# Batch 0's softmax, the fused weights and the weight conversions of a fused attention and feed-forward kernel get due times of their own

## The chip, the cores and the metric

The kernel runs on one core of a Trainium2 chip. The metric is the device time of one launch in microseconds (us), inputs and output in DRAM; all is computed in float32 precision. A core has TensorE (PE), VectorE (DVE), ScalarE (ACT), GpSimd (POOL), and SyncE (SP), which issues all transfers here; DMA engines carry them.

## The reference

```python
def _attn_ref(q, k, v, tau) -> np.ndarray:          # (4, 6080, 256)
    qn = q / (np.linalg.norm(q, axis=1, keepdims=True) + 1e-06)
    kn = k / (np.linalg.norm(k, axis=1, keepdims=True) + 1e-06)
    s = kn.transpose(0, 2, 1) @ qn / tau
    s = s - s.max(-1, keepdims=True)
    a = np.exp(s)
    a /= a.sum(-1, keepdims=True) + 1e-09
    return (v @ a).astype(np.float32)
...
    h = x @ w_in                                     # 256 -> 2048
    h2 = h * h
    h3 = h2 * h
    P = a[0] + a[1] * h + a[2] * h2 + a[3] * h3
    Q = 1.0 + np.abs(b[0]) * np.abs(h) + np.abs(b[1]) * h2
    g = P / (Q + 1e-06)
    return (g @ w_out).astype(np.float32)            # 2048 -> 256
```

The attention is over channels: for each of four batches the scores are a 256 x 256 matrix, summed over all 6080 rows of k and q. The result goes through a feed-forward layer whose activation is a quotient of polynomials.

## The kernel before, in words

**Algebra.** The matrix a of a batch is multiplied into w_in first: a *fused weight* is w_in transposed with the exponentials, scaled by the inverse of their sums. With it, v needs one matrix product to the hidden layer. The hidden layer's 2048 columns are worked as eight *pairs* of 2 x 128; so each batch has eight fused weights, each as a high and a low half (tiles w and w2), and each product is three: high x high, high x low, low x high.

**Tokens.** A batch's 6080 rows are 12 *groups*: eleven of 512 tokens and one of 448. For each group v is loaded (vst), transposed on DVE (cv) and split into vhi (ACT) and vlo (POOL). For each group and pair, `pair` then does: first product on PE into a PSUM slot hx (12 matmuls of 512 columns); on ACT the size, its square, the slope, the inverse root and its square; on DVE num, gh (high), back and rest; on POOL gl (low); and on PE the second product into acc with gh (8 matmuls) and gl (4). There are 384 pairs. `finish` transposes acc to orow and stores it.

**Attention.** `Attn` loads k and q in 24 *halves* of a batch (tile kq; in batch 0 also r). Each half gives 8 matmuls on PE and squares on ACT (tile sq), added up on POOL, and in batch 0 every fourth on DVE (the total is in orow for batch 0, in ssq for the others). `softmax` then makes norms of k and q (a matmul with ones), scores, exponentials, transposes, and calls `fuse` for each pair: 8 matmuls into an hx slot, the high half on ACT, the low half on DVE. Batch b + 1's attention runs while batch b's pairs do. Its first `FRONT` halves, for batch 1, have their products in batch 0's opening and one sum in acc.

**Weights.** `piece` turns one of 16 blocks of the float64 weights that are read as words (8 of w_in, 8 of w_out) into float32: a load into d, an absolute value on ACT, and six DVE steps in an hx slot (for w_out a high half on ACT and a low half on DVE besides). Twelve of the pieces are done in the opening.

**Order.** Nothing runs in the order in which it is written. Each `step` has an engine, an estimated cost and a due time (its key); the `Planner` plays all engines through with these costs, and gives an engine that is free the ready step with the lowest key whose buffers are free:

```python
        FIFO = ("d", "uu", "r", "gh", "gl", "w", "kq", "sq", "cv", "vst", "vhi", "vlo", "orow", "acc")
```

Tiles of these names are given out in order of key. The order that comes out is the program order of each engine; the hardware then waits on semaphores, whatever the planner thought. Due times come from two tables: `LAG` gives each operation of a pair an offset for each of the eight pairs, added to the pair's own time `at + p * II` (`II` is 3.576), and `TIME` gives the rest. The numbers are no microseconds of the chip; only their order counts. PSUM holds three hx slots and one acc. All work goes through one helper, so that the trace gives line L56 for all of it; tiles tell what is what.

In the softmax before, all steps of a batch have keys within one unit after `at`, the halves of k and q are evenly spaced, the eight fused weights are 1.116 apart, and a piece's load and conversion are 5.42 apart.

## Time and profile before

| | us |
|---|---|
| median of 3 runs | 2459.4 (2458.28 to 2464.83) |
| the profiled execution | 2459.0 |
| its span (first to last instruction) | 2457.2 |
| PE busy in it | 2370.8 |
| DVE, ACT, POOL busy | 2177.2, 2156.1, 1330.9 |

The span is what the trace covers; 1.8 us of the profiled execution lie around it. A busy PE is not the same as a PE at full clock: a matmul at a lower granted clock is busy for longer. Opening means the time until batch 0's pairs run evenly, about the first 217 us; the changes of batch lie near 680, 1270 and 1860 us.

### The profile page before, as it was taken

Reading aid. Unit: us, or ns where it says so; the run is one execution under the profiler, and the core shown is the slowest. Engines: PE = TensorE matmul, PEld = TensorE weight load, DVE = VectorE, ACT = ScalarE, POOL = GpSimd, SP = SyncE. Lnnn points to the kernel's source line nnn. Section 1 sums busy time; section 2 is a strip of 40 time slices with the busy share of each in tenths; the row PEclk is TensorE's granted clock in tenths of the full one; section 3 lists DMA queues with packets and bytes.
Section 4 is the critical chain, followed back from the end, with each engine's and each line's share of the span. In section 5 each row is a group of like instructions: output and inputs, shape, how many; then the busy total and the mean of one; then the engine's idle time right before and its main releaser. Section 6 shows DMA issues by size and latency. Waiting matters only on the chain. (4 is left out here: it accounts for less than half of the span.)

```text
span 2457.2 us, 29203 instructions
## 1 busy us (share of the span) xinstructions
PE 2370.8 (96%) x10280; PEld 1939.5 (79%) x10280; DVE 2177.2 (89%) x1953; ACT 2156.1 (88%) x2187; POOL 1330.9 (54%) x525
## 2 busy tenths in 40 slices
PE   8789999999989999999999999999999999999997
PEld 6667888888877888888878788888887778888886
DVE  7779999999978888899987888899998899999997
ACT  5488999999888888899988888889997999999996
POOL 6566555554536666554544666655553345455553
PEclk9889999999999999999999999999999999999999
DMA  9532111111112222311111223211111111111101
GB/s 315 158 106 52 22 22 26 27 25 18 26 17 52 56 56 72 72 25 18 26 18 17 61 52 77 67 18 26 25 27 18 17 26 26 18 27 26 25 9 18
DMA packets 457037, 110.04 MB, mean 45 GB/s; under 512 B 405168, under 2 KB 453808, under 8 KB 456880
## 3 DMA queue, kind: packets, MB, share of 16 engines
q1 hardware_dynamic: 456880, 108.07, 20.1%
q8 instruction: 83, 1.36, 0.2%
q14 instruction: 74, 0.61, 0.1%
HBM read 83.10 MB, written 24.90 MB: 44 GB/s over the span
## 5 line engine op out<-in xcount | busy, mean ns | idle before, releaser
L56 POOL TENSOR_TENSOR gl<-d,r 128x1024 fp32r<-128x1024 f32 (+1 forms) x384 | 957.1, 2496 | 989.2 <-DVE d L56 561.7
L56 PE MATMUL hx<-vhi,w 128*128 128x512 f32 (+1 forms) x3072 | 894.2, 393 | 7.1 <-DVE d L56 6.9
L56 PEld LDWEIGHTS hx<-vhi,w 128*128 128x128 f32 x3072 | 575.7, 188 | 141.6 <-DVE d L56 9.0
L56 DVE SCALAR_TENSOR_TENSOR hx<-uu,fit,hx 128x1024 f32<-128x1024 f32 (+1 forms) x384 | 488.0, 1271 | 89.0 <-ACT uu L56 88.7
L56 DVE SCALAR_TENSOR_TENSOR gh<-hx,fit,r 128x1024 fp32r<-128x1024 f32 (+1 forms) x384 | 485.1, 1263 | 76.3 <-ACT r L56 73.1
L56 DVE SCALAR_TENSOR_TENSOR d<-d,gh 128x1024 f32<-128x1024 f32 (+1 forms) x384 | 525.9, 1370 | 2.6
L56 ACT ACTIVATE d<-hx 128x1024 f32<-128x1024 f32 (+1 forms) x384 | 388.7, 1012 | 156.7 <-PE hx L56 134.2
L56 PE MATMUL acc<-gh,w_high 128*128 128x512 f32 (+1 forms) x1536 | 482.8, 396 | 14.7 <-DVE gh L56 10.6
L56 DVE SCALAR_TENSOR_TENSOR d<-hx,fit,d 128x1024 f32<-128x1024 f32 (+1 forms) x384 | 485.3, 1264 | 6.7
L56 PE MATMUL hx<-vlo,w 128*128 128x512 f32 (+1 forms) x1536 | 478.6, 393 | 0.0
L56 PE MATMUL acc<-gh,w_low 128*128 128x512 f32 (+1 forms) x1536 | 476.1, 391 | 0.0
L56 ACT ACTIVATE uu<-hx,fit 128x1024 f32<-128x1024 f32 (+1 forms) x384 | 457.4, 1191 | 0.0
L56 ACT ACTIVATE d<-d,fit 128x1024 f32<-128x1024 f32 (+1 forms) x384 | 437.4, 1140 | 0.0
L56 ACT ACTIVATE r<-d 128x1024 f32<-128x1024 f32 (+1 forms) x384 | 403.6, 1052 | 26.3 <-ACT d L56 0.8
L56 PE MATMUL acc<-gl,w_high 128*128 128x512 f32 (+1 forms) x1536 | 407.8, 392 | 2.9 <-POOL gl L56 2.9
L56 ACT ACTIVATE r<-r 128x1024 f32<-128x1024 f32 (+1 forms) x384 | 402.2, 1048 | 5.3
L56 PEld LDWEIGHTS acc<-gh,w_high 128*128 128x128 f32 x1536 | 289.6, 189 | 77.6 <-DVE gh L56 13.0
L56 PEld LDWEIGHTS acc<-gl,w_high 128*128 128x128 f32 x1536 | 288.0, 188 | 68.5 <-POOL gl L56 5.3
L56 PEld LDWEIGHTS acc<-gh,w_low 128*128 128x128 f32 x1536 | 290.7, 189 | 61.7
L56 PEld LDWEIGHTS hx<-vlo,w 128*128 128x128 f32 x1536 | 288.9, 188 | 63.8
L56 POOL TENSOR_TENSOR ssq<-sq,ssq 128x1024 f32<-128x1024 f32 (+1 forms) x69 | 186.7, 2706 | 82.2 <-ACT sq L56 80.3
L56 POOL TENSOR_TENSOR vlo<-cv,vhi 128x1024 fp32r<-128x1024 f32 (+1 forms) x48 | 149.4, 3112 | 18.5 <-ACT vhi L56 18.5
(107 smaller groups left out, 1017.5 us busy)
## 6 DMA issues: line engine op xcount, KB each, us to landing
vst<-in_v_dram SPq DMA_DIRECT2D x352, 64.0 KB, 2.4
out_dram<-orow SPq DMA_DIRECT2D x352, 64.0 KB, 1.9
kq<-in_k_dram SPq DMA_DIRECT2D x78, 256.0 KB, 3.5
kq<-in_q_dram SPq DMA_DIRECT2D x78, 256.0 KB, 4.1
d<-in_moe_w_in_dram SPq DMA_DIRECT2D x8, 512.0 KB, 6.3
r<-in_k_dram SPq DMA_DIRECT2D x10, 256.0 KB, 5.8
r<-in_q_dram SPq DMA_DIRECT2D x10, 256.0 KB, 6.1
d<-in_moe_w_out_dram SPq DMA_DIRECT2D x4, 512.0 KB, 6.8
```

Of the source, the lines that this page charges most:

```text
L56: ins = op(*args, **kwargs)
```

## The change

1. The numbers of `LAG` and `TIME` are others. New entries give a due time to each piece's load and each piece's conversion (`piece_load`, `piece`), to each fused weight (`fuse0` in batch 0, `turn` in the others), to each step of the softmax (`chain0`, `chain`), to the first v (`value0`), and an offset to each pair of the first group (`first`), of the first group of a later batch (`opening`) and of the last group of a batch (`last`).
2. `FRONT` goes from 12 to 6: of batch 1's halves, six instead of twelve have their products in the opening.
3. In `softmax` the DVE step that folded the two sums of squares into one is gone; PE does the norms of both sums and adds them in PSUM. The maximum, y and the corrected norms stay in PSUM (nps); scores and exponentials are written into the tile of the squares' sum instead of two sq slots; the transposed exponentials (eT) and rk have buffers of their own. Tiles n2 and y are gone.
4. Costs that the planner takes for these steps are others.

Of the tables, a few lines stand for all.

```diff
...
-    "high": (-0.201, -1.824, -3.214, 1.127, -2.441, -0.333, -0.417, 2.742),
...
+    "high": (22.59291, 24.11209, 24.41897, 24.49546, 24.51312, 23.95582, 24.16201, 24.16013),
...
-    "out0": -1.882, "out": -2.395, "attn0_0": -6.63, "attn_0": 0.275, "attn0": 6.33, "attn": 1.996,
-    "attn1": 92.175, "value": 148.575, "fuse": 1.116, "finish": 72.482, "front": 29.573,
...
+    "pair": 3.576, "start": 175.73828, "load": 0.04809, "softmax": 4.9627, "in": 5.42,
...
+    "attn0": 6.54104, "attn": 0.29516, "attn1": 93.92602, "value": 201.67145, "finish": 125.06256,
+    "front": 75.0448, "front_pace": 13.10818,
...
+    "fuse0": (167.64562, 152.54228, 165.11912, 148.87503, 168.34446, 172.36125, 175.0073, 179.5675),
+    "turn": (-37.56063, -0.4301, -46.60573, 6.0525, 1.56793, 0.10546, 5.12072, 16.26872),
+    "first": (-0.04097, -23.90782, -16.14628, -4.63735, -4.34016, -4.78556, -4.65507, -5.66606),
+    "last": (-1.36381, -1.49737, 4.25864, -3.87953, 4.30997, 4.5312, -4.86916, 2.06908),
+    "opening": (1.54538, 7.26692, 6.40396, 11.04622, 3.47761, -3.70507, -6.7909, -1.11722),
...
+    "value0": -8.75639, "ahead": 49.0606, "vhi": -95.57053, "vlo": 79.4786,
...
-    FRONT = 12
+    FRONT = 6
...
-              "n2": C + NC2, "s0": C + NC2, "y": C + NC2, "e": C + NC2}
+              "s0": C + NC2, "e": C + NC2, "rk": NC2, "eT": 2 * C}
...
+                chain = TIME["chain" if b else "chain0"]
                 nps = buf("hx", [P, 2, GT], F32, "norms")
-                n2, s0, y, e = (buf(t, [P, W], F32) for t in ("n2", "s0", "y", "e"))
-                rn, rk = (buf(t, [P, W], F32, "r" + t) for t in ("y", "n2"))
+                s0, e = buf("s0", [P, W], F32), buf("e", [P, W], F32)
                 total = self.ssq
 
-                def fold():
-                    dve.tensor_tensor(total[:, : 2 * C], total[:, : 2 * C], total[:, 2 * C :], op=ALU.add)
-
                 def norms_pe():
-                    pe.matmul(nps[:, 0, 0:C], ones, total[:, C : 2 * C], start=True, stop=True, skip_group_check=True)
-                    for i in range(NC2):
+                    for n in range(2):
+                        at = 2 * n * C
                         pe.matmul(
-                            nps[:, 0, C + i : C + i + 1], total[:, i * P : (i + 1) * P], ones[:, 0:1],
-                            start=False, stop=True, skip_group_check=True,
+                            nps[:, 1, 0:C], ones, total[:, at + C : at + 2 * C],
+                            start=n == 0, stop=n == 1, skip_group_check=True,
                         )
-
-                step("DVE", 0.7, at, fold, [total], [total], True)
-                step("PE", 1.7, at, norms_pe, [total], [nps])
-                fn = lambda: dve.tensor_scalar_max(n2.tile, nps[:, 0, :W], 1e-30)
-                step("DVE", 0.45, at + 0.02, fn, [nps], [n2])
-                fn = lambda: act.activation(s0.tile, n2.tile, AF.Abs_reciprocal_sqrt)
-                step("ACT", 0.45, at + 0.03, fn, [n2], [s0])
+                        for i in range(NC2):
+                            pe.matmul(
+                                nps[:, 1, C + i : C + i + 1], total[:, at + i * P : at + (i + 1) * P], ones[:, 0:1],
+                                start=False, stop=n == 1, skip_group_check=True,
+                            )
+
+                step("PE", 1.4, at + chain[1], norms_pe, [total], [nps])
+                fn = lambda: dve.tensor_scalar_max(nps[:, 1, :W], nps[:, 1, :W], 1e-30)
+                step("DVE", 0.45, at + chain[2], fn, [nps], [nps])
+                fn = lambda: act.activation(s0.tile, nps[:, 1, :W], AF.Abs_reciprocal_sqrt)
+                step("ACT", 0.45, at + chain[3], fn, [nps], [s0])
...
-                step("DVE", 4.6, at + 0.04, norms_y, [n2, s0], [y, e], True)
+                    n2, y = nps[:, 1, :W], nps[:, 0, :W]
+                    dve.tensor_tensor(y, n2, s0.tile, op=ALU.mult)
+                    dve.tensor_tensor(e.tile, y, s0.tile, op=ALU.mult)
+                    dve.scalar_tensor_tensor(e.tile, e.tile, 1.0, y, op0=ALU.subtract, op1=ALU.mult)
+                    dve.scalar_tensor_tensor(n2, e.tile, -0.5, y, op0=ALU.mult, op1=ALU.add)
+                    dve.tensor_scalar(e.tile, n2, 1e-6, None, op0=ALU.add)
+
+                step("DVE", 2.4, at + chain[4], norms_y, [nps, s0], [nps, e])
...
-                sn, ex = buf("sq", [P, NC2, C], F32, "sn"), buf("sq", [P, NC2, C], F32, "ex")
+                step("DVE", 1.9, at + chain[5], norms_r, [e], [rn, rk])
+                soft = total
+
+                def view():
+                    return total.tile.rearrange("p (u i c) -> p u i c", u=2, i=NC2)
...
-                step("DVE", 2.8, at + 0.08, scores, [self.scores, rk, rn], [sn, stat])
+                step("DVE", 1.8, at + chain[6], scores, [self.scores, rk, rn], [soft, stat])
...
-                step("ACT", 2.7, at + 0.1, exps, [sn, stat], [ex, stat])
+                step("ACT", 2.4, at + chain[7], exps, [soft, stat], [soft, stat])
...
-                step("DVE", 0.5, at + 0.15, inverse, [stat], [stat], True)
+                step("DVE", 0.6, at + chain[8], inverse, [stat], [stat], True)
                 eps = buf("hx", [P, 2, GT], F32, "exps")
-                eT = buf("sq", [P, NC2, C], F32, "eT")
+                eT = buf("eT", [P, NC2, C], F32, "eT")
...
-                step("PE", 0.7, at + 0.12, turned, [ex], [eps])
+                step("PE", 0.6, at + chain[9], turned, [soft], [eps])
                 fn = lambda: act.copy(eT.tile.rearrange("p j i -> p (j i)"), eps[:, 0, :])
-                step("ACT", 0.6, at + 0.13, fn, [eps], [eT])
-                self.w = [self.fuse(p, at + 1 + TIME["fuse"] * p, eT, stat) for p in range(NFP)]
+                step("ACT", 0.6, at + chain[10], fn, [eps], [eT])
+                self.w = [self.fuse(p, at + TIME["turn" if b else "fuse0"][p], eT, stat) for p in range(NFP)]
...
-                step("ACT", 0.9, at + 0.2, high, [slot, stat], [hi])
-                step("DVE", 0.95, at + 0.3, low, [slot, stat, hi], [lo])
+                step("ACT", 0.9, at + TIME["chain" if self.b else "chain0"][11], high, [slot, stat], [hi])
+                step("DVE", 0.95, at + TIME["chain" if self.b else "chain0"][12], low, [slot, stat, hi], [lo])
...
-        for n, (side, m) in enumerate(EARLY):
-            c = 8.0 + TIME["in"] * n
-            piece(side, m, min(c, 36.0 + 0.1 * n) - 6.0 if side == "in" else c - 6.0, c)
-        late = [("out", m, TIME["out0"] + TIME["out"] * m) for m in range(NFP) if ("out", m) not in EARLY]
-        for n, (side, m, c) in enumerate(sorted(late, key=lambda x: x[2])):
-            piece(side, m, T0 + c - 12.0, T0 + c)
+        pieces = EARLY + [("out", m) for m in range(NFP) if ("out", m) not in EARLY]
+        for n, (side, m) in enumerate(pieces):
+            piece(side, m, TIME["piece_load"][n], TIME["piece"][n])
         attns = [Attn(0, 0.0, TIME["load"], TIME["softmax"])]
-        vparts = [values(0, TIME["softmax"])]
+        vparts = [values(0, TIME["value0"])]
...
-                pair(G * NFP + p, at + p * II, vparts[G], attns[b].w[p], acc)
+                moved = TIME["first"][p] if G == 0 else TIME["opening"][p] if g == 0 else TIME["last"][p] if g == NG - 1 else 0.0
+                pair(G * NFP + p, at + p * II + moved, vparts[G], attns[b].w[p], acc)
```

**DVE, from batch 0's last sum of squares to its norms.** hx, d and uu are the tiles of a piece's conversion, w_low its low half, orow the sum of squares, n and y tiles of the norms, e the corrected norms. Before (the last add into orow stands 18 rows ahead of the first of these):

```order
L56 SCALAR_TENSOR_TENSOR hx_70<-d_72,hx_70 128x512
L56 SCALAR_TENSOR_TENSOR w_low<-hx_69,fit,w_high 128x512
L56 TENSOR_SCALAR hx_70<-hx_70 128x512
L56 SCALAR_TENSOR_TENSOR uu_78<-d_72,hx_70 128x512
L56 TENSOR_TENSOR hx_70<-uu_78,hx_70 128x512
L56 SCALAR_TENSOR_TENSOR hx_70<-uu_78,hx_70 128x512
L56 TENSOR_TENSOR orow_108<-orow_108 128x512
L56 SCALAR_TENSOR_TENSOR w_low<-hx_70,fit,w_high 128x512
L56 TENSOR_SCALAR n_111<-hx_69 128x258
L56 COPY sacc_109<-acc_71 128x512
L56 STREAM_TRANSPOSE cv_110<-vst_103 128x1024
L56 TENSOR_TENSOR y_113<-n_111,s_112 128x258
```

Of the change, beginning with that last add:

```order
L66 TENSOR_TENSOR orow_110<-sq_100,orow_110 112x1024
L66 TENSOR_TENSOR hx_70<-uu_78,hx_70 128x512
L66 SCALAR_TENSOR_TENSOR hx_70<-uu_78,hx_70 128x512
L66 SCALAR_TENSOR_TENSOR uu_77<-d_75,hx_69 128x512
L66 TENSOR_TENSOR hx_69<-uu_77,hx_69 128x512
L66 SCALAR_TENSOR_TENSOR w_low<-hx_70,fit,w_high 128x512
L66 SCALAR_TENSOR_TENSOR hx_69<-uu_77,hx_69 128x512
L66 TENSOR_SCALAR hx_70<-hx_70 128x258
L66 SCALAR_TENSOR_TENSOR w_low<-hx_69,fit,w_high 128x512
L66 TENSOR_SCALAR hx_69<-d_74 128x512
L66 COPY sacc_111<-acc_71 128x512
L66 TENSOR_TENSOR hx_70<-hx_70,s_113 128x258
```

Before, 23 rows of conversions stand between the last add and the fold (the row orow<-orow), and PE's norms come behind that. Now six stand between the add and the first step on the norms (hx_70<-hx_70, 128x258).

**PE, batch 0's softmax.** hx<-kq are products of k and q (of batch 1 here, two rows of four matmuls each half), hx<-ident the transposes of the exponentials, hx<-w_in_sb a fused weight (two such rows of four matmuls), hx<-vhi and hx<-vlo the first pair. Before:

```order
L56 MATMUL hx_69<-kq_97 128x256 x4
L56 MATMUL hx_69<-kq_98 128x256 x4
L56 MATMUL hx_70<-ident,sq_101 128x128 x4
L56 MATMUL hx_68<-w_in_sb,sq_100 128x256 x4
L56 MATMUL hx_69<-w_in_sb,sq_100 128x256 x4
L56 MATMUL hx_70<-w_in_sb,sq_100 128x256 x4
L56 MATMUL hx_68<-w_in_sb,sq_100 128x256 x4
L56 MATMUL hx_69<-w_in_sb,sq_100 128x256 x4
L56 MATMUL hx_70<-w_in_sb,sq_100 128x256 x4
L56 MATMUL hx_68<-w_in_sb,sq_100 128x256 x4
L56 MATMUL hx_69<-w_in_sb,sq_100 128x256 x4
L56 MATMUL hx_70<-vhi_104,w_87 128x512 x2
```

Of the change:

```order
L66 MATMUL hx_68<-kq_96 128x256 x4
L66 MATMUL hx_68<-kq_97 128x256 x4
L66 MATMUL hx_69<-ident,orow_110 128x128 x4
L66 MATMUL hx_69<-kq_98 128x256 x4
L66 MATMUL hx_69<-kq_99 128x256 x4
L66 MATMUL hx_69<-w_in_sb,eT_102 128x256 x4
L66 MATMUL hx_70<-w_in_sb,eT_102 128x256 x4
L66 MATMUL hx_69<-kq_96 128x256 x4
L66 MATMUL hx_69<-kq_97 128x256 x4
L66 MATMUL hx_68<-vhi_106,w_88 128x512 x2
L66 MATMUL hx_68<-vlo_108,w_88 128x512 x2
L66 MATMUL hx_68<-vhi_106,w_117 128x512 x2
```

Before, eight fused weights follow the transposes, then the first pair. Now there is a half of k and q, two fused weights, a half, and the first pair; the other six fused weights stand among pairs and halves.

**ACT, the change to batch 2.** d<-hx is the first of a pair's steps, uu, r and r<-r the others; the row with sm is the exponentials (sm holds their maxima and sums), and the copy from hx that of the transposed ones. Before:

```order
L56 ACTIVATE d_72<-hx_69 128x2x448
L56 ACTIVATE uu_78<-hx_69,fit 128x2x448
L56 ACTIVATE d_72<-d_72,fit 128x2x448
L56 ACTIVATE r_81<-d_72 128x2x448
L56 ACT_TABLE_LOAD
L56 ACTIVATE sq_101,sm_115<-sq_100,sm_115 128x256 x2
L56 ACTIVATE r_81<-r_81 128x2x448
L56 COPY sq_100<-hx_70 128x512
```

Of the change:

```order
L66 ACTIVATE d_74<-hx_69 128x2x448
L66 ACTIVATE r_81<-d_75 128x2x448
L66 ACTIVATE uu_76<-hx_69,fit 128x2x448
L66 ACTIVATE r_81<-r_81 128x2x448
L66 ACTIVATE d_74<-d_74,fit 128x2x448
L66 ACT_TABLE_LOAD
L66 ACTIVATE ssq_104,sm_115<-ssq_104,sm_115 128x256 x2
L66 ACT_TABLE_LOAD
L66 ACTIVATE r_79<-d_74 128x2x448
L66 ACTIVATE d_72<-hx_68 128x2x448
L66 ACTIVATE r_79<-r_79 128x2x448
L66 ACTIVATE uu_78<-hx_68,fit 128x2x448
```

Before, the exponentials come behind the steps of the old batch's last pair (hx_69). Now they come behind those of the last but one (hx_69 there), and the last pair (hx_68) follows them. From the first product of the pair that they come behind to the transposes there are 12 matmuls on PE before, 44 now.

## Rows read from the trace of the kernel before

**Rows 1.** Page, part 1: busy us of each engine, share of span, instructions.

```profile
PE 2370.8 (96%) x10280; PEld 1939.5 (79%) x10280; DVE 2177.2 (89%) x1953; ACT 2156.1 (88%) x2187; POOL 1330.9 (54%) x525
```

**Rows 2.** Windows: us, PE, PEld, DVE, ACT, POOL busy; clock; DMA share; GB/s.

```profile
...
0.00:216.60 216.60, 173.03 (x711) 140.37 (x712) 175.16 (x246) 138.33 (x161) 133.03 (x60) 0.92 0.58 174
216.60:660.00 443.40, 442.06 (x1920) 359.59 (x1919) 414.98 (x341) 420.03 (x411) 232.85 (x90) 1.00 0.15 25
660.00:720.00 60.00, 53.85 (x246) 46.06 (x245) 48.15 (x62) 46.11 (x61) 27.01 (x12) 0.97 0.11 18
720.00:1265.00 545.00, 540.51 (x2359) 441.54 (x2357) 485.27 (x398) 491.10 (x484) 313.55 (x121) 1.00 0.21 45
```

**Rows 3.** PE's waits, whole span: total us, times, longest us.

```profile
...
PE hx L56 <- DVE d L56: 19.6, 16, 2.5
PE hx L56 <- ACT sq L56: 18.7, 6, 7.4
PE acc L56 <- DVE gh L56: 10.6, 4, 7.8
```

**Rows 4.** PE's timeline, opening: start us, us, work, [idle before <-releaser].

```profile
...
87.82 0.59 PE L56 MATMUL hx<-orow,ones 128*128 128x256 f32 x2
...
105.04 1.39 PE L56 MATMUL hx<-ident,sq 128*128 128x128 f32 x4 [7.40 <-ACT sq L56]
107.17 15.85 PE L56 MATMUL hx<-w_in_sb,sq 128*128 128x256 f32 x64 [0.73 <-ACT sq L56]
...
139.21 1.22 PE L56 MATMUL acc<-gh,w_high 128*128 128x512 f32 x2 [7.81 <-DVE gh L56]
...
181.19 3.62 PE L56 MATMUL hx<-kq 112*128 112x256 f32 x16
184.46 0.82 PE L56 MATMUL acc<-gh,w_high 128*128 128x512 f32 x2
```

**Rows 5.** POOL's timeline, opening.

```profile
...
58.24 7.24 POOL L56 TENSOR_TENSOR orow<-sq,orow 128x1024 f32<-128x1024 f32 x3 [1.40 <-DVE orow L56]
...
93.64 2.35 POOL L56 TENSOR_TENSOR vlo<-cv,vhi 128x1024 fp32r<-128x1024 f32 x1 [1.52 <-ACT vhi L56]
```

**Rows 6.** DVE's timeline, opening.

```profile
...
65.93 1.22 DVE L56 TENSOR_TENSOR orow<-sq,orow 112x1024 f32<-112x1024 f32 x1
...
82.44 2.60 DVE L56 TENSOR_TENSOR orow<-orow 128x512 f32<-128x512 f32 x1
84.96 0.74 DVE L56 SCALAR_TENSOR_TENSOR w_low<-hx,fit,w_high 128x512 fp32r<-128x512 f32 x1
...
93.74 2.53 DVE L56 SCALAR_TENSOR_TENSOR e<-e,s 128x258 f32<-128x258 f32 x1
96.31 2.47 DVE L56 SCALAR_TENSOR_TENSOR e<-y,e 128x258 f32<-128x258 f32 x1
```

**Rows 7.** DVE's timeline, first change of batch.

```profile
...
671.90 0.43 DVE L56 SCALAR_TENSOR_TENSOR e<-e,s 128x258 f32<-128x258 f32 x1
```

**Rows 8.** ACT's timeline, first change of batch.

```profile
...
680.07 0.92 ACT L56 ACTIVATE d<-hx 128x896 f32<-128x896 f32 x1 [0.42 <-PE hx L56]
```

**Rows 9.** PE's timeline, first change of batch.

```profile
...
685.91 0.33 PE L56 MATMUL hx<-ident,sq 128*128 128x128 f32 x1 [3.48 <-ACT sq L56]
...
688.13 1.11 PE L56 MATMUL acc<-gh,w_high 128*128 128x448 f32 x2 [1.17 <-DVE gh L56]
```

**Rows 10.** PE's waits from 720 to 1265 us.

```profile
...
PE hx L56 <- DVE d L56: 3.1, 3, 1.9
```

**Rows 11.** Groups of POOL from 720 to 1265 us: busy us, mean ns.

```profile
...
L56 POOL TENSOR_TENSOR gl<-d,r 128x1024 fp32r<-128x1024 f32 (+1 forms) x90 | 225.6, 2509 | 216.5 <-DVE d L56 133.7 <-ACT d L56 41.4 <-PE acc L56 34.7
L56 POOL TENSOR_TENSOR ssq<-sq,ssq 128x1024 f32<-128x1024 f32 (+1 forms) x20 | 56.5, 2825 | 13.3 <-ACT sq L56 12.7
```

**Rows 12.** Page, part 6: DMA issues, KB each, us from issue to landing.

```profile
kq<-in_q_dram SPq DMA_DIRECT2D x78, 256.0 KB, 4.1
```

**Rows 13.** POOL's timeline, batch 1.

```profile
...
836.26 3.50 POOL L56 TENSOR_TENSOR ssq<-sq,ssq 128x1024 f32<-128x1024 f32 x1 [2.94 <-ACT sq L56]
```

52 lines of the change are left out of this document (25 added, 27 removed).

## The prediction

> **What bounds the kernel now.** First the busy line of the page: TensorE (PE) is busy 2370.8 of 2457.2 us, and no other engine comes near [rows 1]. So the time is PE's work plus what PE loses, and the change can only touch the loss. The view by stretches says where that is [rows 2]: from 216.6 to 660 us PE is busy 442.06 of 443.40 (1920 matmul records, 0.2302 us each, at a granted clock of 1.00, which is the level of 2.4 GHz), while the first 216.6 us hold 43.6 us of idleness at a mean granted clock of 0.92, and the 60 us around the first change of batch lose 6.15, at a clock of 0.97. The list of PE's waits names the reasons [rows 3]: squares and exponentials (ACT sq), a slot of hx (DVE d), and gh. Outside these places nothing is to be had.
>
> **PE's work is nearly constant.** The same 384 pairs, 96 halves of k and q and 32 fused weights are done. Only the norms grow: without the fold, PE does two sets instead of one per batch. The two long records of batch 0's set at 87.82 show 0.59 us [rows 4]; four more sets are **+2.4** (with their four short records between 2 and 3.2). The four folds were DVE work.
>
> **The opening.** I measure loss as time minus work. Before, by 216.6 us: 711 records, of which 48 halves and 8 fused weights make 448. 16 of these take from 181.19 to the next row at 184.46, 0.204 each [rows 4]; in the opening I take 0.21, so 94.1 us. 252 records of pairs at 0.2302 are 58.0, the rest about 2: work 154.1, loss 62.5.
>
> Now the changed order, walked with durations of these rows. The chain of squares sums (POOL three adds, DVE one) sets the pace: 7.24 us for three adds, then 1.40 until POOL goes on [rows 5]. Before, its last add started at 65.93 [rows 6]. In the new order v and vlo come first and the fourth add stands behind five conversions of a weight whose load is third behind v; I put the landing near 22 from the loads around it, an estimate that may be 4 us off, and with five conversions of 0.74 [rows 6] the add near 26. Five rounds of 7.24 + 1.40 later the last one ends at 69 to 71, some 3 us later than before. But then DVE did w_out conversions until the fold at 82.44 [rows 6], and PE had the sums only at 87.82 [rows 4]. Now six such conversions stand between, and there is no fold: norms on PE at 74. From there to the transposes at 105.04 it was 17.2 us before. Two of DVE's five short steps in it took 2.53 and 2.47 us [rows 6], the first of them beside POOL's vlo [rows 5], against 0.43 for such a step in batch 1 [rows 7]; the new steps work on PSUM and stand beside no vlo, so I take 4.2 off, 13: transposes at 87.
>
> First fused weight: 92 instead of 107.17 [rows 4]. First pair, held by DVE's low half of its weight: 102 instead of 122.7, where the row of fused weights ends (107.17 + 15.85 less the overlap). PE has then done 38 halves and 2 fused weights (70 us, loss 32); before, 40 halves and 8 (83 us, loss 39.5). So only 7.5 of these 20 us are gained there, since six fused weights are still to do.
>
> After it the rest of the loss before is 62.5 - 39.5 = 23: the 7.81 us wait for gh at 139.21 [rows 4], the hx waits and the slow clock behind both. In the new order two halves or a fused weight stand between pairs and give ACT and DVE the time. Walking on, PE waits 0.7 at the fifth fused weight, 5.4 around 171 to 181 where ACT falls behind (62 ACT rows between first pair and ninth, 63 us at 420.03/411 = 1.02 each [rows 2], against 67 of PE work, so little is spare where several stand together), and 3.9 for a slot of hx near 190: 10, plus some slow clock, 12 or so. Loss 44 to 45 in all. **Term: -17.** Bounds: -3 if after the first pair PE waits as long as before and the loads are 4 us late; -28 if it doesn't wait there at all.
>
> **The three changes of batch.** Before, the transposes wait 3.48 us for the exponentials [rows 9], and for batches 2 and 3 the same wait stands again: the 18.7 of [rows 3] are 7.4 and 0.7 in batch 0 [rows 4], then three times about 3.5. Batch 1's norms now stand behind the eighth pair, and its exponentials some 80 pairs ahead of use: that wait goes. For batches 2 and 3 ACT's exponentials stood behind the steps of the outgoing batch's last pair, now behind those of the last but one. So between the first product that they come after and the transposes PE has 12 records before, 44 now (2.4 and 8.9 us, 448 of 512 columns at 0.2302). ACT needs from that product's end the steps of a pair, the table and the exponentials: from 680.07 [rows 8] until the transposes could start at 685.91 [rows 9] it took 5.8 with most of one pair; the pair before that stands mixed in makes it about 8.3. I leave them 1 us each: -8.5. The gh waits (1.17 [rows 9], and of the 10.6 in all that leave 7.81 and 1.17 out 1.6 more) go, since by a count of the order the shortest distance from first product to gh rises from 6.7 to 8.6 us of PE work: -2.8. The clock, 0.97 over the 60 us around the change [rows 2], costs up to 1.8 each; with shorter waits I take 3 of these 5.4 back. **Term: -14.** Bounds -5 (the waits move to the fused weights) and -21.
>
> **Inside batches 0 to 2.** In 720 to 1265, batch 1, PE waits 3.1 us for slots of hx [rows 10] of its 4.5 idle us [rows 2], at products of k and q; batch 2 has the same products. The shortest distance between uses of a slot there rises from 9.8 to 13.0 us of work. **-4** (0 to -6). In exchange these products now come within some 14 pairs. From the adds of half 4 to those of half 17, POOL has 14 adds and 4 gl: 14 x 2.825 + 4 x 2.509 [rows 11] = 49.6, and 5.1 for a load of 4.1 [rows 12] and a square of 1.02 ahead of them; PE has 56.6 us of work to the last products meanwhile. It just fits: **+2** for two batches, bounds 0 and +23 (rival C).
>
> **Elsewhere.** The offsets of all pairs change, but the spacing of first product, gh and slot in the body is the same (10.2 and 13.0 to 13.9 us at the shortest), so nothing; the tail's last products and sums stand at the same distance: nothing, within 1 us.
>
> **Sum.** 2459.0 (the profiled execution; the median is 2459.4) - 17 - 14 - 4 + 2.4 + 2 = **2428**.
>
> **Rivals.** (A) The opening gives nothing: the head start is eaten because the squares of halves 22 and 23 stand behind a w_out piece's absolute value on ACT, and by ACT after the first pair. For it: two more pieces now stand before those squares in SP's queue. Against: DVE's w_out stretch before the fold is gone in any case. 2459 - 14 - 4 + 4.4 = 2445.
>
> (B) More than forecast: no waits after the first pair, clean batch changes: 2459 - 28 - 21 - 6 + 2.4 = 2406.
>
> (C) POOL bounds the dense stretch of products. An add has taken 3.50 us [rows 13]; if all 18 operations do, 63 + 5.1 against 56.6 holds PE 11.5 us, twice: 2428 - 2 + 23 = 2449. The Trainium skill, "SBUF — State Buffer", section "SBUF: two separate sides", says that the port pair of VectorE and GpSimd is an exclusive lock, and that a VectorE instruction with two SBUF inputs blocks a reading GpSimd instruction for its whole length; every pair has such a step (back). By that rule each add that meets one pays it whole, and the longest row fits; the mean of 2.825 says that few do.
>
> (D) No change: fused weights spread among pairs hold a slot of hx until DVE has made the low half, and each of 24 costs a pair 0.7 us, the wait that I found once: +17, and the opening gives 3: 2459 - 3 - 14 - 4 + 4.4 + 17 = 2459. That would also be the reading if a list of due times changes the order but not the critical resources.
>
> (E) Slower: the new offsets order the body worse. About 320 pairs lie outside the stretches above; PE's idleness in 216.6 to 660 is 1.34 us for 80 pairs. At 0.1 us more per pair the gain is gone; at 0.15 it is 2428 + 48 = 2476. Against: the unchanged spacing.
>
> **Chances.** Forecast (2418 to 2440) 0.51, A 0.17, B 0.12, C 0.06, D 0.10, E 0.04. This kernel's change can be told from none beyond 0.3% (7 us): faster 0.86 (forecast, A, B, C), same 0.10 (D), slower 0.04 (E). Range 2410 to 2450: it leaves out half of B, and D and E. The forecast's own range is 2418 to 2440.
>
> **What would show it.** Right: norms on PE near 74 us, first pair near 102, idleness of PE in the opening down to 30, no wait for ACT sq at the first batch change, and 216.6 to 600 as full as before. Wrong: a last add after 75, PE waiting at loads of k and q in the dense stretch, or small hx waits in every pair.

## The result and the profile after

The changed kernel takes 2433.15 us (2430.78 to 2434.55, four runs) against 2460.45 (2458.28 to 2464.83) for the kernel before: ratio 0.9886, 95% interval 0.9869 to 0.9903. The profiled execution took 2430.78 with a span of 2429.0. The total lies 5 us from the forecast of 2428 and inside its own range. The terms do not: the opening, forecast at -17, gave nothing, and the changes of batch and the stretches inside batches gave more than forecast.

The busy line of the page, to be read against [rows 1]: PE has 7.1 us less of busy time, and is idle for 65.3 us instead of 86.4.

```profile
PE 2363.7 (97%) x10304; PEld 1943.4 (80%) x10304; DVE 2170.6 (89%) x1952; ACT 2158.6 (89%) x2187; POOL 1323.5 (54%) x525
```

The windows (us, busy PE, PEld, DVE, ACT, POOL, granted clock, DMA share, GB/s) answer [rows 2]:

```profile
0.00:216.60 216.60, 177.50 (x727) 144.36 (x728) 174.94 (x259) 138.74 (x166) 124.30 (x58) 0.94 0.59 174
...
100.00:240.00 140.00, 126.71 (x525) 103.09 (x526) 124.57 (x140) 109.90 (x126) 68.64 (x28) 0.94 0.30 76
...
300.00:640.00 340.00, 340.00 (x1474) 276.00 (x1473) 318.78 (x261) 323.31 (x315) 179.44 (x69) 1.00 0.15 24
640.00:700.00 60.00, 60.00 (x287) 53.11 (x286) 53.06 (x52) 50.57 (x61) 39.39 (x16) 1.00 0.17 27
700.00:1245.00 545.00, 543.66 (x2377) 445.93 (x2376) 488.07 (x402) 500.79 (x495) 311.24 (x120) 1.00 0.21 45
1245.00:1305.00 60.00, 57.10 (x268) 50.41 (x267) 48.18 (x64) 46.20 (x63) 27.42 (x12) 0.97 0.14 22
...
1842.00:1902.00 60.00, 57.10 (x261) 49.63 (x260) 46.63 (x59) 47.92 (x62) 18.16 (x9) 0.97 0.11 17
```

The first change of batch has no idle time left where 6.15 us stood, and a clock of 1.00. The second and third keep 2.90 each at 0.97; before, they had this:

```profile
1265.00:1325.00 60.00, 54.41 (x239) 45.92 (x240) 44.39 (x60) 47.01 (x62) 27.80 (x12) 0.94 0.10 17
```

The opening holds 16 more matmul records in the same 216.6 us, and 39.1 us of idle time instead of 43.6: that is all that this window shows of the forecast's large term. Of PE's waits in the whole span (total, times, longest) the one for the exponentials (ACT sq, 18.7 us in [rows 3]) is gone; the first two and the last here stand in the opening and at the changes:

```profile
PE hx L66 <- DVE d L66: 11.5, 6, 3.3
PE acc L66 <- DVE gh L66: 7.2, 3, 2.7
...
PE hx L66 <- DVE sacc L66: 4.6, 1, 4.6
```

**Where the 28 us came from.** A stretch of a fixed clock time holds different work in the two kernels, so I compare at equal work: the start of the n-th of the pairs' 9,216 matmuls, less all PE work that the program has ahead of it, at 0.2302 us for 512 columns, 0.2014 for 448, 0.2045 for 256 (costs as in [rows 2, 4]). What is left is the loss up to there, good to about 1 us, since the few other matmuls are priced roughly; the end is that of PE's last matmul. Matmul 1900 lies before the first change, 2400 behind it; 4400 and 4704, 6700 and 7008 enclose the second and third.

```
loss (us) at pair matmul   100   300   600  1900  2400  4400  4704  6700  7008   end   work
before                    57.9  65.2  65.5  66.0  77.6  84.6  96.6 106.1 117.8 127.1  2319.8
changed                   51.9  63.1  67.6  67.6  68.7  71.3  78.3  80.6  87.8  96.5  2322.5
```

| term | forecast | measured |
|---|---|---|
| opening (to 1900) | -17 | +1.6 |
| three changes of batch | -14 | -10.5, -5.0, -4.5: -20.0 |
| inside batches 1 and 2, with dense products | -4 + 2 | -4.4, -7.2: -11.6 |
| the rest to the end | 0 | -0.6 |
| more work (norms) | +2.4 | +2.7 |
| sum | -30.6 | -27.9 |

### The profile page after: what moved, and what is told of

Its sections match the earlier page's. It is cut to its first block, busy times and chain, and to the rows that moved or that the text cites. A ratio compares the mean times of both kernels' runs of the same rounds, so it can differ in the third digit from the quotient of the medians.

```text
span 2429.0 us, 29283 instructions
## 1 busy us (share of the span) xinstructions
PE 2363.7 (97%) x10304; PEld 1943.4 (80%) x10304; DVE 2170.6 (89%) x1952; ACT 2158.6 (89%) x2187; POOL 1323.5 (54%) x525
## 4 chain that ended last, share of the span: by engine, by line
PE 91%; DVE 3%; ACT 2%; POOL 2%; issue 1%; DMA 1%; SPq 0%; DVEq 0%; POOLq 0%; ACTq 0%
PE hx L66 49%; PE acc L66 42%; POOL orow L66 1%; DVE hx L66 1%; ACT r L66 1%; ACT d L66 1%; DVE d L66 1%; DVE gh L66 1%; DVE orow L66 0%; SPq L66 0%; ACT uu L66 0%; DMA r<-in_k_dram 0%; DMA d<-in_moe_w_in_dram 0%; ACT L66 0%; DVE sm L66 0%
## 5 line engine op out<-in xcount | busy, mean ns | idle before, releaser
L66 DVE SCALAR_TENSOR_TENSOR d<-d,gh 128x1024 f32<-128x1024 f32 (+1 forms) x384 | 519.0, 1352 | 2.4
L66 PEld LDWEIGHTS acc<-gh,w_low 128*128 128x128 f32 x1536 | 289.7, 189 | 61.1
L66 POOL TENSOR_TENSOR ssq<-sq,ssq 128x1024 f32<-128x1024 f32 (+1 forms) x69 | 180.2, 2612 | 37.1 <-ACT sq L66 30.4
L66 POOL TENSOR_TENSOR vlo<-cv,vhi 128x1024 fp32r<-128x1024 f32 (+1 forms) x48 | 154.9, 3228 | 21.4 <-ACT vhi L66 21.3
```

The source lines that it names most:

```text
L66: ins = op(*args, **kwargs)
```

## Experiments

The kernel that is edited is the changed one, unless another is named, and each run was compared with the kernel before in the same series (medians 2460.95 to 2461.13). The first five undo one part of the number tables each, or all of them, one more follows up what they showed, and the others try what bounds the opening.

### The opening's numbers, or the changes' numbers, as before

```diff
-    FRONT = 6
+    FRONT = 12
...
-    "front": 75.0448, "front_pace": 13.10818,
+    "front": 29.573, "front_pace": 2.529,
-    "fuse0": (167.64562, 152.54228, ...
+    "fuse0": (1.000, 2.116, ...
-    "first": (-0.04097, -23.90782, ...
+    "first": (0, 0, ...
-    "chain0": (0, -104.53519, ...
+    "chain0": (0, 0, 0.02, ...
```

(and the pieces 5.42 apart, `load`, `softmax`, `value0` and the due time of the first v's load as before)

> The changed kernel with the opening's numbers of before: twelve halves of batch 1 in the opening, evenly spaced loads and conversions of weights, batch 0's softmax and fused weights one after the other, first v at its old due time; the new softmax code, the changes of batch and the body stay new. Theory 1, from the trace after (the time lost by 240 us of the trace is 62.2 us there against 64.6 before, with 2 us more of norms in it): the new opening gave next to nothing, so this runs within 5 us of the changed kernel's 2433, and its trace shows a first change of batch without a wait of over 1 us. Theory 2, the prediction's own term: the opening gave 17 us, so this runs at about 2450.

2450.72 (2447.85 to 2452.32), ratio 0.9957 [0.9942, 0.9971]: 17.5 us slower than the changed kernel. PE's timeline has the norms even earlier than in the changed kernel, since there is no fold in either; but the window from 100 to 240 us has 456 matmul records where the changed kernel has 525. First the row of PE's timeline, then the window:

```profile
71.51 0.70 PE L66 MATMUL hx<-orow,ones 128*128 128x256 f32 x2 [1.18 <-DVE orow L66]
```

```profile
100.00:240.00 140.00, 115.31 (x456) 92.11 (x454) 103.16 (x115) 90.86 (x105) 60.70 (x24) 0.89 0.30 80
```

The time is the one that theory 2 gives, but not for its reason. The loss at matmul 1900 is 81.2: 13.6 above the changed kernel, and 15.2 above the kernel before, whose numbers for the opening these are. Undoing a part does not give back what the part brought: the old numbers of the opening do badly beside the new ones of the body (with the old ones, in a run below, the loss at 300 is 60.2 instead of 76.1). Against the kernel before, the new opening has earned nothing.

```diff
-    "turn": (-37.56063, -0.4301, -46.60573, ...
+    "turn": (1.000, 2.116, 3.232, ...
-    "last": (-1.36381, ...
+    "last": (0, ...
-    "opening": (1.54538, ...
+    "opening": (0, ...
-    "chain": (0, -10.98043, -54.8154, ...
+    "chain": (0, 0, 0.02, ...
```

(and `attn1`, from which the softmax's due times are counted, as before)

> The changed kernel with the due times of before for softmax and fused weights of batches 1 to 3, and no offsets for the first and last group of a batch; opening, body and code stay new. Theory 1: the three changes of batch gave about 20 us (their 60 us windows lose 6.15, 5.59, 5.59 us of idleness before and 0.00, 2.90, 2.90 after, and the slow clock behind each wait besides), so this runs at 2448 to 2456, with waits of about 3.5 us ahead of the transposes. Theory 2: the new body offsets alone clear these waits, since they set when the old batch's last pairs give up slots; then it runs at 2433 to 2438.

2456.62 (2454.41 to 2459.3), ratio 0.9981 [0.9971, 0.9991]: 23.5 us slower than the changed kernel, more than the 20.0 that the table gives the changes. The losses at the three changes are 8.7, 6.8 and 12.2 (1.1, 7.0 and 7.2 in the changed kernel), and those inside batches 1 and 2 are 9.0 and 7.0 instead of 2.6 and 2.3; the opening stays within 0.8. PE's timeline at the first change shows waits where the changed kernel has none:

```profile
715.57 1.08 PE L66 MATMUL acc<-gl,w_high 128*128 128x448 f32 x4 [1.59 <-POOL gl L66]
...
719.33 0.71 PE L66 MATMUL hx<-vhi,w 128*128 128x512 f32 x2 [2.68 <-DVE d L66]
```

What theory 1 looks for, waits of about 3.5 us ahead of the transposes, does not come back at any change. This is the second:

```profile
1290.43 0.60 PE L66 MATMUL hx<-ident,ssq 128*128 128x128 f32 x4
```

So beside the new body these rows of the table are needed for the gain at the changes, and they set part of the loss inside the batches as well. That they took away the wait for the exponentials is not shown: without them it is gone too, and other waits stand in its place.

### The pace of k and q, the body's offsets, and all numbers as before

```diff
-    ... "attn0_0": -5.38831, "attn_0": 0.21848,
-    "attn0": 6.54104, "attn": 0.29516, ...
+    ... "attn0_0": -6.63, "attn_0": 0.275,
+    "attn0": 6.33, "attn": 1.996, ...
```

> The changed kernel with the old due times of the halves of k and q of batches 1 to 3 (spread over the batch instead of dense). Theory 1: the spread products cost the waits for slots of hx inside batches 1 and 2 (4.49 us of idleness each before, 1.34 after) and the slow clock behind them, so this loses 4 to 12 us against 2433. Theory 2: these waits came from the old pair offsets and the pace is indifferent, 2433 within 3 us.

2596.81, ratio 1.0556 [1.0539, 1.0574]. That is beyond anything expected. The loss grows by 68 us inside batch 1 and 78 inside batch 2, where the products of k and q stand. PE's largest waits in the whole span:

```profile
PE hx L66 <- DVE d L66: 71.5, 30, 6.6
...
PE acc L66 <- DVE orow L66: 36.6, 13, 3.4
```

```diff
 LAG = {
-    "size": (-14.90945, ...
+    "size": (-27.601, ...
     ...
-    "low": (290.85324, ...
+    "low": (160.09, ...
...
-    ... "value": 201.67145, "finish": 125.06256,
+    ... "value": 148.575, "finish": 72.482,
```

(all rows of `LAG` but `full`, thirteen, and `ahead`, `vhi`, `vlo`)

> The changed kernel with all old offsets of the operations of a pair and the old due times of v and of the stores; opening, changes of batch and pace of k and q stay new. Theory 1, the prediction's: the body is as good in either order, as PE loses only 1.3 us from 216 to 660 us before, so this runs at 2433 within 5 us. Theory 2: numbers of the changes of batch and of the body belong together, and the waits come back where both meet, 2440 or more, with the added waits within 30 us of a change of batch. Against both: small waits in every pair, 2470.

2653.70, ratio 1.0780 [1.0762, 1.0798]. The loss is again far above every expectation, and it is of another kind: PE waits at second products for gh, 21 times.

```profile
PE acc L66 <- DVE gh L66: 139.3, 21, 11.6
```

Then all numbers of the kernel before, with the new code alone:

```diff
-    "size": (-14.90945, ...
+    "size": (-27.601, ...
 ...
-    FRONT = 6
+    FRONT = 12
 ...
-        pieces = EARLY + [("out", m) for m in range(NFP) if ("out", m) not in EARLY]
...
+        for n, (side, m) in enumerate(EARLY):
+            c = 8.0 + TIME["in"] * n
...
```

> The code of the change (norms of both sums on PE, norms in PSUM, own buffers, no fold) with every due time, offset and number of halves as before. Theory 1, from the run with the old opening (norms at 71.5 us there against 87.82 before, lost time at 125 us 36.3 against 42.4): without the fold, PE has batch 0's sums 16 us earlier, but only some 6 us of it arrive behind the first pair; 2450 to 2457. Theory 2, the prediction's split: the fold was what the head start of the opening hung on, and this alone gives most of 17 us, 2443. Theory 3, from the two runs with mixed numbers (2597 and 2654): numbers fit one code only, so the old ones with the new code run slower than before, over 2465.

2619.48, ratio 1.0645 [1.0627, 1.0663]. Up to matmul 300 it is no worse than either kernel (loss 60.2), then it loses 107.6 us by matmul 1900 in a body that costs both kernels 5 at most. Window and waits of PE from 240 to 640 us:

```profile
240.00:640.00 400.00, 332.55 (x1342) 252.84 (x1341) 320.46 (x238) 300.74 (x287) 152.42 (x63) 0.98 0.12 19
```

```profile
PE hx L66 <- DVE d L66: 49.7, 28, 2.7
```

No engine is full there. So I looked at what an order gives the other engines as time. The *lead* of a pair is the PE work in the program between the end of its first product and the start of its second with gh: in this time ACT, DVE and POOL must do the whole chain of the pair. It is read from the order of PE's instructions, priced as above (mean over pairs, us):

```
pairs                 0-10  10-20  20-40  40-60  60-80
before                12.1   18.5   18.6   19.0   18.6
changed               18.4   14.6   18.5   19.0   18.6
e1_opening_old        11.3   12.4   14.7   19.0   18.6
e4_body_old           14.3   12.5   14.7   19.0   18.6
e5_code_alone         11.3    6.6    6.2    6.3    6.2
```

A pair is 5.5 us of PE work (24 matmuls of 0.2302), so a lead of 18 to 19 is the work of more than three pairs, one of 6 that of little more than one, and in e5 it doesn't build up again through the batch. The test: keep everything of that kernel, and let only the first products of the first twelve pairs fall due earlier, 12 due times in all.

```diff
-                step(eng, cost * s, at + LAG[name][p], fn, reads, writes, port)
+                step(eng, cost * s, at + LAG[name][p] - (10 if name == "in" and m < 12 else 0.0), fn, reads, writes, port)
```

> The code of the change with all old numbers, as in the run that took 2619 us, but for one: the first products of the first 12 pairs are due 10 units earlier. By a count of PE's program, the work that stands between the end of a pair's first product and its first gh product, in pairs 20 to 80, is then 14.7 to 19.0 us on average, against 6.2 in the run of 2619, and 18.5 to 19.0 in both the kernel before and the changed one. Theory 1: this lead, which the opening builds up or not and the body keeps, decides the body; with it, PE loses under 15 us between 240 and 640 us of the trace instead of 90, and the run is 75 or more below 2619. Theory 2: the body of that run is slow by its offsets with the new code (the step back took 1.68 us there beside POOL's gl, against 1.32), and 12 due times change nothing: within 20 us of 2619.

2478.89 (2477.83 to 2482.7), ratio 1.0068 [1.0052, 1.0085]: 140.6 us below the kernel with the numbers alone. The lead becomes 12.2, 12.5, 14.7, 19.0, 18.6, and the same window and wait of PE read

```profile
240.00:640.00 400.00, 396.71 (x1710) 321.25 (x1709) 373.08 (x305) 379.78 (x370) 208.98 (x81) 1.00 0.15 24
```

```profile
PE hx L66 <- DVE d L66: 2.9, 2, 1.9
```

The code is the same, so the numbers made the 107.6: twelve due times take it away. That they act through the lead is what its return and the waits say; the order of the other engines changes with them, and was not held fixed. The lead doesn't explain the two runs before. In batch 0, e4's is like e1's from the tenth pair on, and its waits for gh have another cause. That of e3 is 14 to 15 in pairs 0 to 20 and 60 to 80 of batches 1 and 2, where the changed kernel has 20.5 and 18.6, which goes with its waits but was not tested by itself. Why the old offsets make PE wait for gh stays open.

### What bounds the opening

The rows of the opening in the changed kernel. First SP's queue and DVE's timeline, then PE's:

```profile
12.37 6.14 SPq L66 DMA_DIRECT2D vst<-in_v_dram  x8
18.55 1.44 SPq L66 DMA_DIRECT2D d<-in_moe_w_in_dram  x3
```

```profile
26.34 0.69 DVE L66 TENSOR_SCALAR acc<-d 128x512 uint32<-128x512 uint32 x1 [4.54 <-DMA d<-in_moe_w_in_dram]
...
29.85 1.22 DVE L66 TENSOR_TENSOR orow<-sq,orow 128x1024 f32<-128x1024 f32 x1
...
73.17 1.23 DVE L66 TENSOR_TENSOR orow<-sq,orow 112x1024 f32<-112x1024 f32 x1 [1.00 <-POOL orow L66]
...
83.17 0.42 DVE L66 SCALAR_TENSOR_TENSOR e<-e,hx 128x258 f32<-128x258 f32 x1
...
86.72 2.17 DVE L66 TENSOR_SCALAR rk<-s,rtau 128x2 f32<-128x2 f32 x1
...
94.82 1.40 DVE L66 TENSOR_SCALAR sm<-sm 128x2 f32<-128x2 f32 x1
...
96.46 2.20 DVE L66 TENSOR_SCALAR sm<-sm,fit 128x2 f32<-128x2 f32 x1
```

```profile
77.88 0.67 PE L66 MATMUL hx<-orow,ones 128*128 128x256 f32 x2 [1.43 <-DVE w_low L66]
...
94.45 0.63 PE L66 MATMUL hx<-ident,orow 128*128 128x128 f32 x4 [0.41 <-DVE w_in_sb L66]
...
104.08 5.41 PE L66 MATMUL hx<-w_in_sb,eT 128*128 128x256 f32 x16 [4.61 <-DVE sacc L66]
...
112.64 0.81 PE L66 MATMUL hx<-vhi,w 128*128 128x512 f32 x2
...
142.00 3.68 PE L66 MATMUL hx<-w_in_sb,eT 128*128 128x256 f32 x8 [3.07 <-DVE d L66]
...
209.63 0.72 PE L66 MATMUL hx<-vhi,w 128*128 128x512 f32 x2 [3.29 <-DVE d L66]
```

The loads of three pieces are issued behind v's eight, and the one that DVE needs lands at 26.34, so the fourth add, behind five conversions on DVE, starts at 29.85; the long steps of the norms take 0.42 now, but three steps with two columns take 2.17, 1.40 and 2.20. Both were tried: the loads first, the two-column steps away from POOL, and both together.

```diff
-    "piece_load": (63.98723, 63.6249, 54.31828, 63.73004, 64.18892, ...
+    "piece_load": (-59.8, -59.9, 54.31828, -60.0, -59.7, ...
...
-            step("DVE", one, c, low_bits, [raw], [work], port)
+            step("DVE", one, c, low_bits, [raw, third], [work], port)
```

(`third` is written by the first add of squares that DVE does)

> The changed kernel; the loads of the four pieces that are converted first go ahead of the first v, and DVE's first add of squares is made a condition of the first conversions and of v's transpose, so that it stands ahead of them. In the trace after, that add starts at 29.85 us behind five conversions whose load landed at 26.3, and the last of the chain at 73.17. Theory 1: the chain of sums sets batch 0's softmax; norms come at 64 to 72 us instead of 77.9, the time lost by 100 us falls by 5 or more from 42.6, and the run is 3 to 8 us below 2433, if the body behind isn't disturbed. Theory 2: the loads set it (DMA engines are busy 0.90 of the first 100 us): norms no earlier than 75, no gain.

2453.13, ratio 0.9966 [0.9954, 0.9977]: slower than the changed kernel by 20.0. The fourth add comes only 1.5 us earlier: ACT's absolute value of a piece is now ahead of the squares in ACT's program and waits for its load, so POOL's third add comes late, and DVE's fourth with it.

```profile
18.25 0.68 ACT L66 ACTIVATE uu<-d 128x512 f32<-128x512 f32 x1 [8.05 <-DMA d<-in_moe_w_in_dram]
```

```profile
28.36 1.23 DVE L66 TENSOR_TENSOR orow<-sq,orow 128x1024 f32<-128x1024 f32 x1 [15.56 <-POOL orow L66]
```

The last add starts at 77.78 instead of 73.17 all the same. The split of the first v now stands between POOL's adds (39.10), and two of DVE's adds stand behind conversions that wait 1.82 and 3.46 for their loads, so that two rounds of the sums take 12.1 and 11.3 us instead of 8.7. The norms come at 82.41 instead of 77.88. Most of the loss is later, though: 75.5 at matmul 300 and 82.1 at 600, 14.5 above the changed kernel, where the planner has ordered pairs 0 to 20 with less lead (17.4 and 12.1 instead of 18.4 and 14.6).

```diff
-                    dve.tensor_scalar_mul(rk[:, :NC2], rn[:, C:], rtau)
...
+                    dve.tensor_scalar(e[:, C:], n2[:, C:], 1e-6, coef[:, 6:7], op0=ALU.add, op1=ALU.mult)
...
-                    dve.tensor_scalar_add(stat[:, 2 * NC2 : 3 * NC2], stat[:, 2 * NC2 : 3 * NC2], 1e-9)
...
+                    dve.tensor_scalar(spare[:, 0:NC2], stat[:, 2 * NC2 : 3 * NC2], 1e-9, inv, op0=ALU.add, op1=ALU.mult)
```

(the temperature is multiplied into the norms ahead of the reciprocal, and both steps write to or read from PSUM)

> The changed kernel without three of the softmax's shortest DVE steps: tau is multiplied into the norms that stand in PSUM ahead of the reciprocal, and the sum of exponentials is scaled into PSUM by the inverse scale, then inverted; no step of two columns goes from SBUF to SBUF any more there, but for one maximum. In the trace after these three took 2.17, 1.40 and 2.20 us beside POOL's adds, where a reciprocal of two columns took 0.17. Theory 1: they stood waiting for POOL; the new ones take 0.2 to 0.5 us each and the stretch from norms to transposes falls from 16.6 by about 2. The first fused weight waited for a slot of hx besides (4.61 us, DVE's conversions), so the time is 2433 within 3. Theory 2: such short steps cost 2 us by themselves in this stretch, and nothing moves. A gain of over 4 us would say that the softmax chain, not DVE's conversions, sets the first pair.

2434.61 (2432.65 to 2438.1), ratio 0.9893 [0.9877, 0.991]: no difference from the changed kernel. DVE's timeline shows why the gain is small: the edited steps take 0.21, and the wait goes to the next such step that was left as it was, at the row maximum (sm<-sm), which took 0.31 in the changed kernel.

```profile
85.67 0.21 DVE L66 TENSOR_SCALAR e<-hx,coef 128x2 f32<-128x2 f32 x1
...
90.28 2.32 DVE L66 TENSOR_SCALAR sm<-sm 128x2 f32<-128x2 f32 x1
...
96.78 0.21 DVE L66 TENSOR_SCALAR hx<-sm,fit 128x2 f32<-128x2 f32 x1
```

The first pair starts at 109.42 instead of 112.64, and the opening is 2.0 better at matmul 1900 (65.6 against 67.6). The changes lose that again: about 10 at the second and third instead of 7, and 1.4 more at the first. It is the edit in batches 1 to 3 that costs there, since a run below with batch 0's alone has 7 at both. The two edits together:

> The two edits together (earlier sums, and no short steps from SBUF to SBUF). Theory 1: gains of the chain add up, norms at 64 to 72 us and the first pair 6 to 10 us ahead of 112.6; 2423 to 2430. Theory 2: DVE's conversions set the first fused weight whatever the chain does, first pair no earlier than 109, 2433 within 4. Since each edit changes what the planner finds free, the body may come out in another order, worse by some us; the lost time at 125 and 217 us (45.3 and 62.2 after) tells the opening apart from that.

2455.22, ratio 0.9975 [0.9965, 0.9984]. The loss at the hundredth pair matmul is 45.8, lower than in any run here but e9 (42.6); at 600 it is 74.7. As with the first edit, what the opening gains up to its first pairs is lost behind them.

So both were tried again so that the planner's order elsewhere stays: the second edit for batch 0 only, and the first by moving steps by hand in the finished order of the first 35 us, which leaves PE's program as it is.

```diff
-                    dve.tensor_scalar(e.tile, n2, 1e-6, None, op0=ALU.add)
+                    if b:
+                        dve.tensor_scalar(e.tile, n2, 1e-6, None, op0=ALU.add)
+                        return
...
```

> The changed kernel with the edit on the short steps (tau and the scale by way of PSUM) in batch 0 alone, so that the changes of batch keep their order. In the run with the edit in all batches the opening came out 2.0 us ahead and the lead was lost at the second and third change of batch. Theory 1: the 2 us stay, 2429 to 2433. Theory 2: a gain in the opening is eaten by the waits for slots behind it, 2433 or more. The changed kernel itself has run at 2430.78 to 2434.55.

```diff
-        return plan.order()
+        done = plan.order()
...
+        sums = [at["sq", 0, 0], at["sq", 0, 1], at["add", 0, 1], ..., at["add", 0, 3], at["sq", 0, 4]]
+        put([s for s in sums], [first])
...
+        put([*third, at["v", 0]], [first])
...
+        return done
```

> The changed kernel in its own planned order, with a few steps of the first 35 us put elsewhere by hand: the loads of the first three pieces ahead of v, the squares and sums of the first halves ahead of all conversions, v's transpose behind the first piece, its split and the first late piece's absolute value behind later sums. PE's program is the same row by row, so the lead is. Theory 1: the chain of sums sets batch 0's softmax; its last add starts at 62 to 67 us instead of 73.17, norms at 66 to 72 instead of 77.88, and the run ends 4 to 9 us below the changed kernel. Theory 2: the loads are the bound (DMA engines busy 0.90 of the first 100 us), the squares then wait for k and q, norms at 76 or later and no gain. Theory 3: norms come early and DVE's conversions hold the first fused weight all the same, gain under 3 us.

> Both edits: the steps of the first 35 us moved by hand, and batch 0's short steps by way of PSUM; PE's program as in the run with the latter alone. Theory 1: the gains add up, 2420 to 2427. Theory 2: only one of them is on the path to the first pair, within 2 us of the better of the two runs.

| | us | ratio | loss at 100, 300, 600, 1900, end |
|---|---|---|---|
| changed | 2433.15 | 0.9886 [0.9869, 0.9903] | 51.9, 63.1, 67.6, 67.6, 96.5 |
| e10, steps | 2429.35 (2428.86 to 2429.99) | 0.9868 [0.9851, 0.9884] | 49.5, 62.1, 66.6, 66.9, 95.5 |
| e11, sums | 2431.10 (2428.86 to 2432.94) | 0.9877 [0.9861, 0.9894] | 49.9, 61.1, 65.6, 65.9, 94.8 |
| e12, both | 2427.57 (2424.95 to 2429.93) | 0.9858 [0.9841, 0.9874] | 50.3, 61.4, 65.7, 66.0, 95.3 |

All three point to a gain, none to a large one; e12 is the fastest kernel of the study, 5.6 us below the changed one by the medians, but the intervals of the ratios still overlap. By the medians the two gains add up (3.8, 2.1 and 5.6 together), by the loss at 1900 they don't (0.7, 1.7 and 1.6). In e10 PE's wait for a slot ahead of the first fused weight falls from 4.61 to 1.61, and the first pair starts at 109.39:

```profile
102.21 3.69 PE L66 MATMUL hx<-w_in_sb,eT 128*128 128x256 f32 x16 [1.61 <-DVE sacc L66]
```

In e11 the fourth add starts 12.8 us earlier, and the last one only 2.1:

```profile
17.09 1.23 DVE L66 TENSOR_TENSOR orow<-sq,orow 128x1024 f32<-128x1024 f32 x1
...
34.78 1.23 DVE L66 TENSOR_TENSOR orow<-sq,orow 128x1024 f32<-128x1024 f32 x1 [0.22 <-ACT sq L66]
...
71.05 1.23 DVE L66 TENSOR_TENSOR orow<-sq,orow 112x1024 f32<-112x1024 f32 x1 [1.02 <-POOL orow L66]
```

because ACT's squares then wait behind the absolute value of a piece whose load lands at 33.06:

```profile
33.06 0.68 ACT L66 ACTIVATE uu<-d 128x512 f32<-128x512 f32 x1 [5.05 <-DMA d<-in_moe_w_in_dram]
```

The late load was taken out of DVE's way and stood in ACT's. The DMA share is 0.90 over the first 100 us in both kernels, which speaks for the loads as the bound of the sums, but only of their start. From 31 us on POOL's adds in the changed kernel wait for DVE's add alone, and a round of four takes 8.66 us (three adds and 1.40; the forecast had 8.64):

```profile
39.87 7.29 POOL L66 TENSOR_TENSOR orow<-sq,orow 128x1024 f32<-128x1024 f32 x3 [1.41 <-DVE orow L66]
```

Neither less to load in this stretch nor another split of the adds between POOL and DVE was tried.

## Why the prediction was right, and where not

**Opening, forecast -17, measured +1.6: the step that failed.** Along the forecast's own points: last add ending 69 to 71, measured 74.4; norms 74, measured 77.88; transposes 87, measured 94.45; first fused weight 92, measured 104.08; first pair 102, measured 112.64; loss behind the first pair 12. The delay grows from 4 to 12 in three steps. (a) The load's landing, 22, was 26.34, which the estimate allowed for, and the fourth add started at 29.85 instead of 26; from there the sums kept the forecast's pace. (b) From norms to transposes 13 was forecast and 16.6 came. The long steps did get as short as forecast, but "stand beside no vlo" was thought of vlo alone: three two-column steps stand beside POOL's adds for batch 1 and take 5.77 in all. Only the first, 2.17, lies in this stretch, and with 0.21 in its place the stretch is no shorter (17.1 in e10, from 78.85 to 95.94). PE's own program fills it: 32 products of batch 1 stand ahead of the transposes, and wait 2.97 and 0.60 for slots of hx. In the changed kernel the exponentials end at 92.4, and the transposes start 2.1 later.

```profile
84.58 5.14 PE L66 MATMUL hx<-kq 128*128 128x256 f32 x16 [2.97 <-DVE e L66]
```

(c) The first fused weight waits 4.61 for a slot of hx that conversions and the copy to sacc hold; it was in no term. Here the other two short steps (3.60) count: they stand ahead of these conversions on DVE, and e10, where they are short, has 3.0 less of this wait.

What the forecast made of this head start failed most. At the start of the first pair the loss, priced as above, is 44.9, and 42.7 in the kernel before: 2.2 more, where 7.5 less was forecast. The first pair comes 10.0 us earlier instead of 20, with 12 us less of PE's work done. From there to matmul 1900 the loss is 22.7, against 23.3 before; 12 was forecast. The waits behind the first pair are near the 10 that were walked through (11.7 in all: 142.00, 209.63, two shorter ones near 190, and one outside the first 217 us). What was mis-sized is the slow clock behind them, 2 in the forecast and some 9 here by the granted clock, whose mean from 112.64 to 300 us is 0.95 (0.86 in the 25 us slice from 175, 0.93 in those from 125, 200 and 250).

```profile
258.22 1.22 PE L66 MATMUL hx<-vhi,w 128*128 128x512 f32 x2 [2.48 <-DVE d L66]
```

The lower bound of the term, "-3 if after the first pair PE waits as long as before and the loads are 4 us late", names what came about: loads 4.3 late, and behind the first pair a loss as large as before. The term lies outside it all the same. Rival A's outcome for the opening holds, for another reason than the one it gives: the sums kept their pace to the last add.

**Changes of batch, forecast -14, measured -20.0: right mechanism, mis-sized clock.** The wait for the exponentials is gone, as forecast; which of the new numbers took it away is open (e2). Idle time in the three windows of 60 us falls from 6.15 + 5.59 + 5.59 to 0 + 2.90 + 2.90, by 11.5; the forecast had 8.5 + 2.8. The clock was taken as 0.97 at all three from the first [rows 2], worth 1.8 each; at the second it is 0.94, worth 3.6, and it rises to 1.00, 0.97 and 0.97. That is 5.4 given back instead of 3 (the third also had 0.94). Some 3 us more are spread over the stretches on both sides. At the second and third change the forecast's 1 us of rest was too little, and it stands at another place: the transposes wait 0.24, the next second product 2.65 for gh.

```profile
1265.13 0.63 PE L66 MATMUL hx<-ident,ssq 128*128 128x128 f32 x4 [0.24 <-DVE d L66]
...
1268.41 1.05 PE L66 MATMUL acc<-gh,w_high 128*128 128x448 f32 x2 [2.65 <-DVE gh L66]
```

**Inside batches, forecast -4 + 2, measured -11.6.** The waits for slots of hx [rows 10] went as forecast: from 700 to 1245 us only 1.3 of idle time is left, and from 1305 to 1842 the same. But each was priced by its length. In the kernel before, one of 1.92 in batch 2 is followed by 16 matmuls in 5.41, where a like group a little later takes 3.62: the wait cost 3.7, not 1.9.

```profile
1365.88 5.41 PE L56 MATMUL hx<-kq 128*128 128x256 f32 x16 [1.92 <-DVE d L56]
...
1379.46 3.62 PE L56 MATMUL hx<-kq 128*128 128x256 f32 x16
```

The rest, some 3 us in batch 2, lies spread in the kernel before and isn't traced. The dense products of k and q cost nothing: no wait for a load or a sum stands from 700 to 1245 us, and POOL's adds there take 2.69 on the mean of 20 [rows 11: 2.825]. Rival C is refuted.

**Norms, forecast +2.4:** +2.7 of work. **Rivals D and E:** fused weights among pairs cost no 0.7 each, and the body is as full as before (340.00 of 340 us busy). But E's mechanism, an order of the body that is worse, is the one that moved most here, in e3, e4 and e5; "the spacing is the same" goes with a lead that is the same from the twentieth pair on.

**Together:** the opening missed by +18.6, the changes by -6.0, inside the batches by -9.6, the rest by -0.3. The total is right by luck: these cancel to +2.7, and the largest term was wrong by more than its size.

## What to carry to other kernels

Numbers of a table that were chosen together don't come apart: undoing one part (17.5 and 23.5 us, and 163 and 220 in the body) measures how badly the old part fits the new rest, not what the new part brought; compare loss at equal work instead. Before pricing single waits in a software pipeline, read from the order how far first products run ahead: a lead that had shrunk to 6 us behind the opening stayed there for the whole batch (e5), while one of 11 to 12 grew back (e1, e9). And an estimate of an opening has to ask of each wait that is removed what is late next, and how much work is not yet done when the next stage starts early: here loads, slots of hx and the slow clock stood behind the waits, and the earlier first pair had 12 us less behind it.
